# The old state added in PSUM by two 128x64 products instead of one 128x128 product

## The chip, the cores and the metric

The kernel runs on one core of a Trainium2 chip. The metric is device time in microseconds (us) of one execution, and the time of a kernel is the median of its runs. The engines are PE (TensorE, matrix products into PSUM; PEld is its loading of the stationary operand), DVE (VectorE), ACT (ScalarE), POOL (GpSimd) and SP (which issues the DMAs). Each engine works through its own list of instructions in order.

## What is computed

A recurrent attention, whose output is the input of two feed-forward blocks, one after the other:

```
for t in range(S):                       # S = 768, 32 heads of 40
    y[:, :, t] = einsum('bhd,bhde->bhe', r_t, state)
    Sa = einsum('bhde,bhe->bhd', state, a_t)
    state = state * w_t - outer(Sa, b_t) + outer(v_t, k_t)
x = y as tokens                          # 3072 x 320
x = leaky(x @ w_in) @ w_out              # width 2048
out = (sigmoid(x @ w_gate) * (x @ w_val)) @ w_out2   # width 1536
```

## The kernel before

**Attention** goes by chunks of 64 steps. Twelve chunks make six blocks `n` of two chunks `ci`; the chunk is `k = 2n + ci`. `q` is one of four batches, with eight heads in it (`i` of four, `h` of two; `h` chooses the lower or upper 64 partitions). For each of the 48 pairs (k, q) the generator `recur` runs one step of the recurrence, and `together` runs two q side by side. A step is a chain across engines, with these lines:

- `fp` (L352): products of the state in FL with r; DVE multiplies them by a mask into W (L355).
- `pm` (L361): eight products of 64 output rows with W; ACT (L365) and DVE (L367) bring them back into W, for each h.
- `yp` (L374, L377, L380): one PSUM tile of 128 partitions by 4 x 104 columns. Columns 40 to 103 are the outputs of the chunk, columns 0 to 39 the new state. L374 adds FL times r (128x64 operands, one for each h, so the product writes 64 of the 128 partitions). L377 adds the old state ST by a product with the whole 128x128 identity into all 128 partitions and 160 columns. L380 adds W times G (128x64 operands, h by turns).
- DVE scales the new state (L384) and writes the outputs y (L395); PE transposes the state (L389), ACT copies it into FL (L391), and ACT and DVE copy it into the next W (L347).

L377 runs when there is a next chunk: 11 chunks by 4 q are 44 of them. All operands are 32-bit floats, and such a product stands in the trace as two passes, so 88.

Around these steps stands other work of the attention: scores `sc` (L190) and transposes `tr` (L216, L225) of the block after the next, the inverses' products `m` (L284, L290) and `qp` (L299), DVE scans `c` and `rc` (L149, L155) of the block after the next. Late in each block, between its last two pairs of steps, DVE transposes the inverse of the next block (`TTc` L262, `Ta` L264) and `Ld` for the one after it (`T` L240); this place is called a block end here; POOL works out the inverses in between.

**The feed-forward blocks** follow. x is loaded (L556, L558) and split into high and low halves `xh`, `xl` on ACT and DVE (L574 to L577). Weights come as 64-bit numbers and are decoded on DVE, ACT and POOL (L510 to L525), beside the products `h` and `o` (L593, L609). The tile x has one buffer, and the decoding of all weights but the first is put behind the output y of (k = 11, q = 2).

The order of instructions on each engine is set by a scheduler that runs over the whole program and goes by its own estimate of each instruction's time. So an edit of one line can move others, on every engine.

Of the kernel before, what the change touches and what calls it, by code (L numbers as in the profile page):

```python
# [18 lines left out]
B, H, S, D = 4, 8, 768, 40  # L19
# [15 lines left out]
def attention(ctx, tc, A, xT, prods):  # L35


    nc = tc.nc
# [8 lines left out]
    ident = const.tile([128, 128], FP32, name="ident")  # L47
# [264 lines left out]
    def bank2(n, name, shape):  # L312
        if n == NB - 1 and name in ('fp',):
            return pa.tile(shape, FP32, tag="pa", name=name)
        return pf.tile(shape, FP32, tag="pf", name=name)
# [3 lines left out]
    def by8(x):  # L319
        return x.rearrange("p e (u x) -> p e u x", x=8)  # L320
# [4 lines left out]
    def recur(n, q, ci):  # L325
# [6 lines left out]
        FL, ST = st["S", k, q]  # L332
# [10 lines left out]
        if more:  # L343
            for h in range(2):
                nc.sync.dma_start(out=W[top[h], h, 0:D // 8], in_=A["v"][h, :, k, q])
            for h in range(2):
                (nc.scalar.copy if h else nc.vector.tensor_copy)(  # L347
                    out=we[own[h].start:own[h].start + ns[h], h, :, 0:D // 8], in_=by8(ST[64 * h:64 * h + ns[h], :, 0:D]))
        fp = bank2(n, "fp", [128, 8, C])
        for h in range(2):  # L350
            for j in range(2):
                nc.tensor.matmul(out=fp[:, 4 * h + 2 * j:4 * h + 2 * j + 2], lhsT=both(FL[:, j, 2 * h:2 * h + 2]),  # L352
                                 rhs=R[:, :, 2 * h + j], start=True, stop=True)
# [6 lines left out]
        for h, i, e in heads:  # L360
            nc.tensor.matmul(out=pm[own[h], i, cols], lhsT=QT[rows[h], 2 * (i // 2) + h, i % 2], rhs=W[rows[h], h, u0:, i],  # L361
                             start=True, stop=True)
# [8 lines left out]
        yp = bank2(n, "yp", [128, 4, X1])  # L371
        for j in range(2):
            for h in range(2):
                nc.tensor.matmul(out=yp[64 * h:64 * h + 64, 2 * j:2 * j + 2, D:X1], lhsT=FL[:, j, 1 + h],  # L374
                                 rhs=R[:, :, 2 * h + j], start=j == 0, stop=False)
        if more:
            nc.tensor.matmul(out=yp[:, :, 0:D], lhsT=ident, rhs=ST[:, :, 0:D], start=False, stop=False)  # L377
        for h, i, e in heads:
            g0 = D * (2 * i + h)
            nc.tensor.matmul(out=yp[64 * h:64 * h + 64, i, cols], lhsT=Gt[:, g0:g0 + 64], rhs=W[:, h, u0:, i],  # L380
                             start=False, stop=i == 3)
# [14 lines left out]
        if ci == 1:  # L396
            for h in range(2):
                nc.sync.dma_start(
                    out=xT.rearrange("(h f e) t -> f e h t", f=2, e=D)[h][:, :, q * S + n * PB:q * S + n * PB + PB],
# [9 lines left out]
    def together(*chunks):  # L409

        todo = [recur(*x) for x in chunks]
        while todo:
            for x in todo:
                for _ in range(4):
                    next(fill[0], None)
            todo = [x for x in todo if next(x, todo) is not todo]
# [500 lines left out]
```

## Time and profile before

| | us |
|---|---|
| median of 3 runs (1250.61 to 1257.71) | 1252.32 |
| the profiled execution | 1257.15 |
| its span, first to last instruction | 1255.4 |
| PE busy in the span | 1149.8 |
| DVE busy in the span | 735.7 |

The attention fills the span up to about 480 us. From there to 600 us the first pass of the first feed-forward block runs, which also decodes weights, and then the rest. The mean granted PE clock is 0.952 of full speed (2.4 GHz); the two levels are 1.2 and 2.4 GHz, so a stretch at 0.90 spent a fifth of its time at the lower one.

### The profile page before, as it was taken

What the parts mean: (1) busy time and instruction counts of PE and PEld (TensorE: products, weight loads), DVE (VectorE), ACT (ScalarE), POOL (GpSimd) and SP (SyncE); (2) the same over time, 40 slices, a digit from 0 to 9 for tenths busy, and PEclk for the clock granted to TensorE, in tenths of its full rate; (3) what the DMA queues carried; (4) which work ended last, traced back from release to release, by engine and by line L of the source; (5) the groups of instructions that cost most, each with busy time, mean ns of one, the idle gap of its engine ahead of it and who ended that gap; (6) DMA issues with size and microseconds to landing.
All of it is one profiled execution on the core that took longest, in us unless ns stands there. A gap on an engine that the chain in (4) does not pass through costs nothing.

```text
span 1255.4 us, 24949 instructions
## 1 busy us (share of the span) xinstructions
PE 1149.8 (92%) x9778; PEld 970.1 (77%) x9778; DVE 735.7 (59%) x1477; ACT 540.2 (43%) x1214; POOL 327.4 (26%) x528
## 2 busy tenths in 40 slices
PE   4749999999999878998999999999999999999997
PEld 3637878787788766876778888877878888888886
DVE  8975667758655247999964444689762323222222
ACT  2334545445454434676653334467651323222221
POOL 6338481845854002444200000022210000000000
PEclk9659899899999887999999999999999999999999
DMA  6503333333322134333420000146850100000000
GB/s 195 172 23 96 95 88 106 80 103 97 92 50 65 29 106 119 93 103 111 124 72 22 26 21 26 43 122 170 186 130 1 46 1 22 1 22 1 21 1 24
DMA packets 121214, 91.08 MB, mean 73 GB/s; under 512 B 57728, under 2 KB 104320, under 8 KB 121088
## 3 DMA queue, kind: packets, MB, share of 16 engines
q1 hardware_dynamic: 121088, 89.40, 26.1%
q8 instruction: 79, 1.29, 0.4%
q14 instruction: 47, 0.39, 0.1%
HBM read 77.57 MB, written 11.80 MB: 71 GB/s over the span
## 4 chain that ended last, share of the span: by engine, by line
PE 66%; DVE 17%; DMA 6%; ACT 4%; issue 4%; SPq 1%; POOL 1%; DVEq 0%; ACTq 0%
PE h L593 18%; PE o L593 9%; PE o L609 9%; PE qp L299 4%; PE pm L361 4%; PE o L716 3%; PE o L717 3%; PE o L718 3%; PE yp L380 3%; PE fp L352 3%; PE sc L190 2%; PE yp L374 2%; DVE c L149 2%; PE m L290 2%; DMA ru<-in_w_val 2%
## 5 line engine op out<-in xcount | busy, mean ns | idle before, releaser
L593 PE MATMUL h<-xh,up 128*128 128x512 f32 x624 | 200.4, 396 | 10.5 <-DVE g L601 8.9
L593 PE MATMUL h<-xl,up 128*128 128x512 f32 x624 | 194.2, 392 | 0.0
L583 ACT CAST gh<-g 128x512 fp32r<-128x512 f32 x168 | 103.9, 619 | 174.1 <-DVE g L729 113.8
L584 DVE TENSOR_TENSOR gl<-g,gh 128x512 fp32r<-128x512 f32 x168 | 122.7, 732 | 71.5 <-ACT gh L583 71.3
L729 DVE TENSOR_TENSOR g<-o,t 128x512 f32<-128x512 f32 x72 | 49.5, 690 | 187.4 <-PE o L593 184.5
L593 PEld LDWEIGHTS h<-xh,up 128*128 128x128 f32 x624 | 115.7, 189 | 38.9 <-DVE g L601 15.5
L593 PEld LDWEIGHTS h<-xl,up 128*128 128x128 f32 x624 | 117.7, 189 | 23.7
L609 PE MATMUL o<-gh,down 128*128 128x512 f32 x450 | 133.3, 390 | 0.2
L525 POOL TENSOR_TENSOR down<-f,e 128x256 fp32r<-128x256 f32 (+2 forms) x41 | 40.8, 1010 | 228.9 <-PE o L609 172.4
L601 DVE TENSOR_TENSOR g<-h,t 128x512 f32<-128x512 f32 x96 | 65.9, 687 | 58.1 <-ACT t L600 57.6
L609 PEld LDWEIGHTS o<-gh,down 128*128 128x128 f32 x450 | 84.5, 188 | 18.6 <-ACT gh L583 1.1
L254 POOL TENSOR_TENSOR T<-T,tmp 128x30 f32<-128x30 f32 (+9 forms) x150 | 92.9, 620 | 10.9
L725 ACT ACTIVATE t<-h 128x512 f32<-128x512 f32 x72 | 42.9, 597 | 121.9 <-PE h L593 121.8
L593 PE MATMUL o<-xh,up 128*128 128x512 f32 x288 | 89.7, 391 | 3.7 <-DVE g L729 1.6
L609 PE MATMUL o<-gl,down 128*128 128x512 f32 x270 | 92.3, 390 | 0.3 <-DVE gl L584 0.2
L249 POOL TENSOR_TENSOR tmp<-T 128x30 f32<-128x30 f32 (+9 forms) x150 | 87.1, 581 | 10.8
L593 PE MATMUL o<-xl,up 128*128 128x512 f32 x288 | 88.6, 389 | 0.0
L600 ACT ACTIVATE t<-h 128x512 f32<-128x512 f32 x96 | 56.9, 592 | 63.0 <-PE h L593 62.8
L525 POOL TENSOR_TENSOR up<-f,e 128x384 fp32r<-128x384 f32 x38 | 46.2, 1216 | 130.9 <-DVE e L519 129.2
L717 PE MATMUL o<-down,gh 128*128 128x320 f32 x264 | 80.3, 308 | 0.0
L716 PE MATMUL o<-down,gh 128*128 128x320 f32 x264 | 80.0, 309 | 0.0
L367 DVE TENSOR_TENSOR W<-pm,masks 64x256 f32<-64x256 f32 x96 | 40.5, 422 | 62.5 <-ACT W L365 60.4
(267 smaller groups left out, 2254.5 us busy)
## 6 DMA issues: line engine op xcount, KB each, us to landing
kb<-in_kb SPq DMA_DIRECT2D x24, 512.0 KB
rd<-in_w_out SPq DMA_DIRECT2D x28, 320.0 KB
w<-in_w SPq DMA_DIRECT2D x24, 260.5 KB
FL<-in_vT SPq DMA_DIRECT2D x96, 64.0 KB
ru<-in_w_in SPq DMA_DIRECT2D x16, 384.0 KB
x<-in_w SPq DMA_DIRECT2D x24, 256.0 KB
ru<-in_w_gate SPq DMA_DIRECT2D x12, 384.0 KB
ru<-in_w_val SPq DMA_DIRECT2D x12, 384.0 KB
```

The lines of the kernel that those rows point to most:

```text
L249: eng.tensor_tensor(out=tv, in0=T[:, i0:i1, j:j + 1].to_broadcast([128, i1 - i0, j]), in1=T[:, j:j + 1, 0:j].to_broadcast([128, i1 - i0, j ...
L254: steps.append(eng.tensor_tensor(out=T[:, i0:i1, 0:j], in0=T[:, i0:i1, 0:j], in1=tv, op=ALU.add))
L299: nc.tensor.matmul(out=qp[:, 2 * j + h], lhsT=X[:, 2 * ci + j, 2 * h:2 * h + 2].rearrange("p a s -> p (a s)"), rhs=tt[:, 4 * h + 2 * ci + ...
L525: nc.gpsimd.tensor_tensor(out=out, in0=f[:, c0:c1], in1=ef[:, c0:c1], op=ALU.mult)
L583: copy = self.nc.scalar.copy(out=gh, in_=g)
L584: self.last = copy.ins, (engine or self.nc.vector).tensor_tensor(out=gl, in0=g, in1=gh, op=ALU.subtract).ins
L593: self.nc.tensor.matmul(out=ps, lhsT=l, rhs=r, start=(i == 0), stop=(i == len(ops) - 1))
L600: self.nc.scalar.activation(out=t, in_=h, func=AF.Copy, scale=0.01)
L601: self.nc.vector.tensor_tensor(out=g, in0=h, in1=t, op=ALU.max)
L609: self.nc.tensor.matmul(out=acc, lhsT=l, rhs=r, start=first and i == 0, stop=last and i == len(ops) - 1)
L716: nc.tensor.matmul(out=o, lhsT=gj, rhs=w[:, 0], start=s, stop=False)
L717: nc.tensor.matmul(out=o, lhsT=gj, rhs=w[:, 1], start=False, stop=False)
```

## The change

The product with the identity is made in two halves: for each h the 64 columns of the identity that give the output partitions 64h to 64h + 63. The values are the same, in the same place of the same accumulation.

```diff
         if more:
-            nc.tensor.matmul(out=yp[:, :, 0:D], lhsT=ident, rhs=ST[:, :, 0:D], start=False, stop=False)
+            for h in range(2):
+                nc.tensor.matmul(out=yp[64 * h:64 * h + 64, :, 0:D], lhsT=ident[:, 64 * h:64 * h + 64], rhs=ST[:, :, 0:D],
+                                 start=False, stop=False)
```

Lines behind the edit have numbers that are higher by two in the changed kernel (L380 is L382 there), and the halves stand on L378. Up to the first of these products the lists of all engines are as before. Behind it the scheduler has moved other instructions, of which three places are shown.

PE, at the two steps of chunk k = 2 with q = 2 and q = 3, in the trace from 208.8 us. `FL_127` and `S_126` belong to one q, `FL_129` and `S_128` to the other; before:

```order
L374 MATMUL yp<-R_119,FL_127 64x2x64 x4
L377 MATMUL yp<-S_126,ident 128x4x40
L380 MATMUL yp<-W,G_101 64x104 x8
L374 MATMUL yp<-R_120,FL_129 64x2x64 x4
L377 MATMUL yp<-S_128,ident 128x4x40
L380 MATMUL yp<-W,G_103 64x104 x8
L216 MATMUL tr<-ident,a_107 128x104 x4
```

and of the changed kernel:

```order
L374 MATMUL yp<-R_119,FL_127 64x2x64 x4
L378 MATMUL yp<-S_126,ident 64x4x40 x2
L382 MATMUL yp<-W,G_101 64x104 x8
L374 MATMUL yp<-R_120,FL_129 64x2x64 x4
L378 MATMUL yp<-S_128,ident 64x4x40 x2
L382 MATMUL yp<-W,G_103 64x104
L216 MATMUL tr<-ident,a_107 128x104 x4
L225 MATMUL tr<-ident,kb 128x104 x4
L382 MATMUL yp<-W,G_103 64x104 x7
```

The halves stand where the whole stood. Behind them transposes have moved in among the products of the second q.

DVE, at the end of the same block (the three long transposes, in the trace from 213.1 us); before:

```order
L264 STREAM_TRANSPOSE Ta<-T 128x32x32
L347 COPY W<-S_122 40x4x5x8
L347 COPY W<-S_132 40x4x5x8
L240 STREAM_TRANSPOSE T<-Ld 128x32x32
L355 TENSOR_TENSOR W<-fp,masks 128x4x8x8 x4
L367 TENSOR_TENSOR W<-pm,masks 64x4x8x8 x4
```

and of the changed kernel:

```order
L264 STREAM_TRANSPOSE Ta<-T 128x32x32
L347 COPY W<-S_122 40x4x5x8
L347 COPY W<-S_132 40x4x5x8
L355 TENSOR_TENSOR W<-fp,masks 128x4x8x8 x2
L240 STREAM_TRANSPOSE T<-Ld 128x32x32
L355 TENSOR_TENSOR W<-fp,masks 128x4x8x8 x2
L367 TENSOR_TENSOR W<-pm,masks 64x4x8x8 x4
```

The mask products of one q have moved ahead of the third transpose. The same holds at three of the block ends (139.6, 213.1 and 350.1 us); at the one at 286.3 us it was so before.

ACT, at the end of the attention (in the trace from 455 us), where the first x is split; before:

```order
L365 ACTIVATE W<-pm 64x4x5x8 x2
L576 CAST xl_7130<-x 64x512
L365 ACTIVATE W<-pm 64x4x5x8
L510 ACTIVATE sq<-rd 128x320
L391 COPY FL_131<-st__6340 128x2x2x40
L574 CAST xh_7129<-x 128x1536
L365 ACTIVATE W<-pm 64x4x5x8
```

and of the changed kernel:

```order
L365 ACTIVATE W<-pm 64x4x5x8 x3
L512 ACTIVATE sq<-rd 128x320
L578 CAST xl_7174<-x 64x512
L393 COPY FL_131<-st__6384 128x2x2x40
L365 ACTIVATE W<-pm 64x4x5x8
L576 CAST xh_7173<-x 128x1536
```

The third and the fourth copy of `pm` each stand ahead of a half of the split that was ahead of them. Further on in that place, the last copy into FL has moved ahead of the split of the second x on ACT, and the last pair of mask products (L355) ahead of it on DVE.

## Rows read from the trace of the kernel before

**Rows 1.** The page, part 4: the chain that ended last, by engine.

```profile
PE 66%; DVE 17%; DMA 6%; ACT 4%; issue 4%; SPq 1%; POOL 1%; DVEq 0%; ACTq 0%
```

**Rows 2.** Busy time by stretch: stretch, length, engines' busy us, PEclk, DMA share, GB/s.

```profile
100.00:480.00 380.00, 343.41 (x5327) 290.16 (x5325) 230.22 (x480) 176.84 (x511) 187.38 (x330) 0.93 0.32 84
480.00:600.00 120.00, 115.14 (x531) 91.94 (x529) 115.12 (x250) 78.73 (x168) 48.35 (x45) 0.97 0.38 108
600.00:1255.00 655.00, 636.78 (x3087) 541.84 (x3086) 305.56 (x534) 252.66 (x441) 41.72 (x36) 1.00 0.19 51
```

**Rows 3.** Timeline of PE, chunk k = 2: start, us, line, operands, passes [idle before].

```profile
208.81 0.61 PE L374 MATMUL yp<-R,FL 128*64 128x128 f32 x8
209.35 0.54 PE L377 MATMUL yp<-S,ident 128*128 128x160 f32 x2
209.81 0.94 PE L380 MATMUL yp<-W,G 128*64 128x104 f32 x16
```

**Rows 4.** The chain in order of time: start, us on the chain, what, passes.

```profile
208.98 0.44 PE yp L374 x8
209.42 0.47 PE yp L377 x2
...
394.52 1.81 PE fp L352 x16
```

**Rows 5.** Timeline of PE where L380 follows L374 with nothing between.

```profile
224.81 0.66 PE L374 MATMUL yp<-R,FL 128*64 128x128 f32 x8
225.30 0.34 PE L380 MATMUL yp<-W,G 128*64 128x104 f32 x2
```

**Rows 6.** Timeline of DVE, chunk k = 2, q = 0: the second half of W.

```profile
172.37 0.42 DVE L367 TENSOR_TENSOR W<-pm,masks 64x256 f32<-64x256 f32 x1 [2.09 <-ACT W L365]
```

**Rows 7.** Timeline of PE at that time.

```profile
172.37 0.54 PE L377 MATMUL yp<-S,ident 128*128 128x160 f32 x2
172.84 0.30 PE L380 MATMUL yp<-W,G 128*64 128x104 f32 x1
```

**Rows 8.** Timeline of DVE at two block ends.

```profile
213.14 2.02 DVE L262 STREAM_TRANSPOSE TTc<-T 128x1024 f32<-128x1024 f32 x1
...
217.45 2.02 DVE L240 STREAM_TRANSPOSE T<-Ld 128x1024 f32<-128x1024 f32 x1
219.29 1.46 DVE L355 TENSOR_TENSOR W<-fp,masks 128x256 f32<-128x256 f32 x4
...
290.64 0.76 DVE L355 TENSOR_TENSOR W<-fp,masks 128x256 f32<-128x256 f32 x2
291.31 2.07 DVE L240 STREAM_TRANSPOSE T<-Ld 128x1024 f32<-128x1024 f32 x1
293.26 0.74 DVE L355 TENSOR_TENSOR W<-fp,masks 128x256 f32<-128x256 f32 x2
```

**Rows 9.** Timeline of PE at the same two block ends.

```profile
219.81 1.26 PE L361 MATMUL pm<-W,QT 104*64 104x104 f32 x16 [0.95 <-DVE W L355]
...
291.12 1.26 PE L361 MATMUL pm<-W,QT 104*64 104x104 f32 x16 [0.75 <-DMA FL<-in_vT]
...
293.72 0.30 PE L361 MATMUL pm<-W,QT 104*64 104x104 f32 x1 [0.32 <-DVE W L355]
```

**Rows 10.** Busy time by stretch, 17 us from the same block ends on.

```profile
213.10:230.10 17.00, 15.70 (x200) 13.40 (x198) 11.82 (x18) 9.32 (x27) 9.34 (x23) 0.90 0.42 121
286.30:303.30 17.00, 14.85 (x230) 12.54 (x229) 14.41 (x24) 11.44 (x32) 8.93 (x19) 1.00 0.47 127
```

**Rows 11.** Timeline of ACT at the end of the attention.

```profile
462.12 0.62 ACT L576 CAST xl<-x 64x512 fp32r<-64x512 f32 x1 [6.07 <-DMA x<-xT]
462.77 0.30 ACT L365 ACTIVATE W<-pm 64x160 f32<-64x160 f32 x1
```

**Rows 12.** Timeline of DVE at the end of the attention.

```profile
478.43 0.69 DVE L577 TENSOR_TENSOR xl<-x,xh 64x512 fp32r<-64x512 f32 x1
479.15 0.76 DVE L355 TENSOR_TENSOR W<-fp,masks 128x256 f32<-128x256 f32 x2
481.85 0.43 DVE L395 TENSOR_TENSOR y<-yp,c 128x256 f32<-128x256 f32 x1 [1.94 <-PE yp L380]
482.19 0.55 DVE L512 SCALAR_TENSOR_TENSOR z<-sq,ru 128x384 f32<-128x384 f32 x1
```

## Prediction

> **What bounds the kernel now.** I read the page's chain of waits first. PE holds 66% of it and DVE 17% [rows 1], so the first question at each place is what PE would do a little earlier. The table by stretch [rows 2] splits the span. The changed product runs only between 100 and 480 us. There PE is busy for 343.4 of 380 us at a mean granted clock of 0.93. From 480 to 600 us PE and DVE are both near full (115 of 120 us each), and the work of both is fixed there, so this stretch should neither give nor take much if it starts earlier. From 600 us on PE alone is full at clock 1.00, and nothing of it is touched. So what is saved before 480 us should reach the end, if PE or what follows from PE ends last where it is saved.
>
> Then I read the timeline and the chain around one of the 44 products. The L377 rows stand on the chain with 0.47 us each [rows 4]. 44 of these are 21 us, of which only a part can go, since the addition itself stays.
>
> **The direct saving.** The neighbours L374 and L380 use the 128x64 form (all rows, half the columns of the array), L377 the whole array. What the form costs is seen in four differences.
>
> - Eight passes of L374, each over 128 columns, hold the chain for 0.44 us, and sixteen of fp (whole array, also 128 columns) for 1.81 us [rows 4]. That is 0.055 against 0.113 us for a pass: passes for the two halves run side by side.
> - From the start of L374 to that of L377 are 0.54 us [rows 3]. The passes explain 0.44, so 0.10 us pass before the array takes the other form.
> - From the start of L377 to that of L380 are 0.46 us [rows 3].
> - Behind an L377, L374 needs 0.49 us until L380 starts [rows 5], 0.05 more than the 0.44 without a change of form ahead of it. I take this for the first weights, whose loading nothing covers.
>
> So where a 128x64 product follows, an L377 costs 0.10 + 0.46 + 0.05 = 0.61 us. Its replacement is four passes of 160 columns in a stream that never changes its form: 4 x 0.055 x 160/128 = 0.28 us. The saving is 0.33 us. Where another form follows (a score, an inverse's product), the leaving costs what entering cost before: 0.56 us become 0.28 + 0.10, and 0.19 is saved. By the new order of PE, 31 of the 44 are followed by a 128x64 product, 11 by a smaller form, and 2 by a whole-array product, where I take nothing. That is 31 x 0.33 + 11 x 0.19 = 12.3 us of PE time.
>
> Not all of it is on the path. At k = 2, q = 0 the second half of W ends at 172.79 us [rows 6] and L380, which reads it, starts at 172.84 [rows 7]. PE could start 0.05 us earlier, and about 0.28 of the 0.33 turns into a wait for DVE. I count five such places by comparing each L380 with its W, and take 1.5 us off: **about 11 us**. As bounds I take 6 (half of the saving turns into such waits) and 13.5 (nothing does, and the few products at the lower clock save twice as much).
>
> The product's operands don't change: ST and the identity are ready where they were ready, no wait is added, and no DMA is moved by the edit itself. PSUM holds the same tile. The 44 extra instructions on PE are in the passes already counted.
>
> **What the new order does.** Three things that I price apart from the saving.
>
> *Block ends.* DVE stands there in three long transposes. In the order before at 213 us, the mask products of both q come behind the third transpose (219.29), and pm waits 0.95 us for them. At 286 us one pair comes ahead of the third transpose (290.64 against 291.31), and pm starts behind it, with 0.75 us of waiting for a DMA and then 0.32 for the other pair [rows 8, 9]. Behind the first kind the granted clock is 0.90 over 17 us, behind the second 1.00 [rows 10]; that is 3.4 us at the lower level, worth up to 1.7 us if PE ends last all that time. The change turns three ends of the first kind into the second. Each can gain nothing (the waits of the second kind are as long) or 0.95 + 1.7 = 2.6 us. I take 1 us each, nearer to the low end because transposes move in among the yp products there too, which puts off y and so the DVE transposes: **3 us**, bounds 0 and 7. The later third transpose delays POOL's inverse by one pair, 0.76 us [rows 8]. In no row does a TTc wait for POOL, so this is free.
>
> *Scans.* At one block the mask products come earlier among the DVE scans than before, and at the next block later. The two are mirror images, and I price them at nothing, with the wait of 0.95 us [rows 9] each way as bounds.
>
> *The handover.* On ACT, a copy of pm stood behind a split that waited 6.07 us for the first x; it ran at 462.77 [rows 11]. On DVE the last mask products stood behind the split of the second x and ran at 479.15, and y, which releases the decoding of the weights, at 481.85 [rows 12]. In the new order both are ahead of the splits. y still stands behind the split of the second x, which ends at 479.12 [rows 12], so this alone gives at most 2.7 us, and an earlier first split, which frees the buffer of x, up to 2 more by my estimate from the queue on ACT. But x must still land, and six lists of instructions have to agree. I take **2 us**, bounds -2 and 5.
>
> **The sum.** 11 + 3 + 2 = 16 us off the profiled execution of 1257.15 us (span 1255.4, and 1.75 us around it): 1241.15. That execution was 0.4% slower than the median of 1252.32; in the same ratio the forecast is 1241.15 x 1252.32 / 1257.15 = **1236 us**. The bounds are 6 + 0 - 2 - 1 = 3 us and 13.5 + 7 + 5 + 1 = 26.5 us off, 1249 and 1226 in medians.
>
> **The rivals.**
>
> *Only the direct saving.* The three effects of order come to nothing, since what waits is moved and not removed, as the DMA wait in [rows 9] shows. 11 us off: 1241.
>
> *PE's time turns into waits.* W is the limit at many more steps than I counted: pm, ACT and DVE make a chain of their own, which the faster PE does not shorten. For it speaks [rows 7], against it the 0.47 us for an L377 on the chain [rows 4]. 3 to 5 us off at the most: 1248.
>
> *The halves don't run side by side, slower.* The two halves read the same ST through the same rows of the array. If each pass ran alone, four would take 4 x 0.113 x 160/128 = 0.57 us, about the 0.56 of now, and if each also had to load its weights with nothing running (0.05 us [rows 5]), 0.77 us. Then a site with a 128x64 successor loses 0.16 us and any other 0.31: 31 x 0.16 + 13 x 0.31 = 9 us slower, 1261 if the order gives nothing. It decides from 0.14 us for each pass on. Against it speaks [rows 4]: the halves of L374 use the same rows of the array, too, and keep 0.055 us, which leaves no room for loads.
>
> The Trainium skill has a rule for this: its page "TensorE: Matmul & The Clock Gate", section "Part 3: Packing small matmuls — row/col tiling", says that weight loads overlap running products only when the row groups differ. By this rule the two column halves would load unhidden, and the time would be this rival's; the L374 rows of this trace disagree.
>
> **How the numbers follow.** Forecast (direct saving and some of the order's) 0.45; only the direct saving 0.30; waits 0.18; halves one by one, or an order that costs more than the saving, 0.07. About 0.5%, 6.3 us, is what a measurement of this kernel can tell from no change. Faster than 1246.1 are the first two cases and a small part of the third, less a part of the second whose direct saving is at its lower bound: 0.77. Slower than 1258.6: 0.05. The rest is 0.18. The range 1227 to 1248 takes in the first two cases with their bounds and the edge of the third.
>
> **What would show it.** In the profile after, each pair of halves should hold the chain for about 0.28 us with no gap before L378 and L382, and its four passes should start two by two. The waits of pm for W (L355) at the three block ends should shrink and the clock there stay at 1.00. The first z of the later weights, at 482.19 us now [rows 12], should start near 466, and the distance from there to the end should stay within 3 us. The prediction is wrong if L378 passes are more than 0.14 us apart, if waits of L382 for W appear for as much as the products lost, or if the feed-forward part gets longer by what the attention gave.

## The result, and the profile after

| | before | after |
|---|---|---|
| median, first comparison | 1251.46 us (4 runs) | 1234.46 us (4 runs) |
| ratio, 95% interval | | 0.9866 [0.9819, 0.9913] |
| the same again on another occasion | 1255.55 us (17 runs) | 1236.25 us (6 runs) |
| ratio, 95% interval | | 0.9858 [0.9812, 0.9905] |
| the profiled execution | 1257.15 us | 1242.24 us |

The changed kernel is faster by 1.3 to 1.4%, clear of the 0.5% that a measurement can tell. The forecast was 1236 us. The two profiled executions differ by 14.9 us. This is where these lie, by stretches that begin and end at the same instructions: the first L374, the first z on DVE (it decodes the first weights), and on ACT the first copy of an output of the first feed-forward block into x2 by L655 (L657 in the changed kernel). [rows 12] ends with another z, the first one of the later weights; the two are kept apart below.

Busy time by stretch of the kernel before (stretch, length, busy us of PE, PEld, DVE, ACT, POOL, then PEclk, DMA share, GB/s):

```profile
100.07:459.96 359.89, 333.81 (x5261) 282.52 (x5259) 218.13 (x454) 169.04 (x495) 185.31 (x327) 0.95 0.32 84
459.96:612.48 152.52, 137.16 (x652) 109.84 (x648) 137.27 (x299) 94.02 (x198) 54.19 (x51) 0.92 0.37 104
612.48:1255.40 642.92, 624.30 (x3032) 531.50 (x3030) 295.49 (x512) 245.16 (x426) 37.89 (x33) 1.00 0.19 51
```

and of the changed kernel:

```profile
106.94:442.60 335.66, 312.63 (x5349) 274.37 (x5347) 220.17 (x454) 168.13 (x496) 191.31 (x327) 0.97 0.34 90
442.60:595.04 152.44, 137.41 (x649) 109.54 (x646) 138.69 (x298) 93.85 (x197) 52.69 (x51) 0.93 0.37 104
595.04:1240.50 645.46, 626.57 (x3035) 534.20 (x3033) 295.42 (x514) 245.76 (x427) 35.98 (x33) 0.99 0.19 50
```

Until the first L374 the changed kernel takes 6.9 us more (106.94 against 100.07), although no instruction has moved there. The recurrence, where the 44 products stand, is 24.2 us shorter at a higher clock. From the first z to the first x2 nothing changes (152.52 and 152.44), and the rest is 2.5 us longer. 6.9 - 24.2 - 0.1 + 2.5 = -14.9.

**The products themselves**, one step of chunk k = 2 and the start of the next, timeline of PE of the changed kernel (start, us, line, operands, passes), to be read against [rows 3]:

```profile
206.37 0.61 PE L374 MATMUL yp<-R,FL 128*64 128x128 f32 x8
206.81 0.44 PE L378 MATMUL yp<-S,ident 128*64 128x160 f32 x4
207.08 0.88 PE L382 MATMUL yp<-W,G 128*64 128x104 f32 x16
207.79 0.61 PE L374 MATMUL yp<-R,FL 128*64 128x128 f32 x8
```

From L374 to the halves are 0.44 us (0.54 before), from the halves to L382 0.27 (0.46 before), and to the next L374 0.71 (0.77 before, 209.81 to 210.58).

**A block end**, the one at 213 us before; DVE and then PE of the changed kernel, to be read against [rows 8, 9] (in brackets the idle time ahead and what ended it):

```profile
215.48 0.76 DVE L355 TENSOR_TENSOR W<-fp,masks 128x256 f32<-128x256 f32 x2
216.15 2.07 DVE L240 STREAM_TRANSPOSE T<-Ld 128x1024 f32<-128x1024 f32 x1
218.13 0.70 DVE L355 TENSOR_TENSOR W<-fp,masks 128x256 f32<-128x256 f32 x2
...
215.96 1.26 PE L361 MATMUL pm<-W,QT 104*64 104x104 f32 x16 [0.71 <-DVE W L355]
218.56 0.30 PE L361 MATMUL pm<-W,QT 104*64 104x104 f32 x1 [0.32 <-DVE W L355]
```

The wait of 0.95 us has become two that are together as long, 0.71 and 0.32. At the other two ends of the first kind one wait of 1.02 and one of 1.01 us became 0.51 and 0.54.

The clock over 17 us at the three block ends of the first kind, of before (the one at 213.1 us is in [rows 10] with 0.90):

```profile
139.60:156.60 17.00, 15.70 (x189) 13.42 (x186) 10.51 (x18) 8.51 (x25) 9.26 (x24) 0.80 0.41 118
350.00:367.00 17.00, 15.63 (x199) 13.35 (x198) 11.31 (x19) 9.37 (x27) 8.97 (x21) 0.90 0.19 45
```

and from the same three ends of the changed kernel on; the fourth row is its end that was of the other kind already (at 286.3 us before, at 274.2 now), and the last row begins 12 us behind the start of that end:

```profile
144.60:161.60 17.00, 16.42 (x251) 14.57 (x249) 15.12 (x26) 11.69 (x33) 8.94 (x19) 1.00 0.52 147
211.20:228.20 17.00, 14.99 (x240) 12.99 (x239) 14.93 (x25) 11.91 (x33) 8.99 (x19) 1.00 0.49 132
339.60:356.60 17.00, 16.40 (x250) 14.55 (x248) 10.84 (x19) 11.61 (x32) 8.39 (x21) 1.00 0.26 67
274.20:291.20 17.00, 16.41 (x250) 14.56 (x249) 15.11 (x26) 11.68 (x33) 8.92 (x19) 1.00 0.52 147
286.30:303.30 17.00, 14.72 (x218) 13.32 (x215) 14.66 (x22) 9.19 (x24) 15.66 (x18) 0.90 0.19 47
```

At all three the clock stays at full speed now. A second trace of the kernel before (r1 below) has it at 1.00, 1.00 and 0.80 over 17 us from the same three ends, so a fall there does not come each time. Over all traces of this document it came at 16 of 19 ends of the first kind, and at 4 of 23 that the new order, or the same exchange by itself, had turned into the second.

The fall in the last row, at 296.4 us, stands in the scans, which the forecast called mirror images. PE's wait for the masks behind them stood at 237.82 us in the kernel before and stands one block later, at 295.69 us, in the changed one (first row before, second after):

```profile
237.82 1.83 PE L361 MATMUL pm<-W,QT 104*64 104x104 f32 x16 [2.55 <-DVE W L355]
...
295.69 1.68 PE L361 MATMUL pm<-W,QT 104*64 104x104 f32 x16 [2.28 <-DVE W L355]
```

**The handover**, DVE of the changed kernel, to be read against [rows 12]:

```profile
458.72 0.42 DVE L397 TENSOR_TENSOR y<-yp,c 128x256 f32<-128x256 f32 x1
459.06 0.55 DVE L514 SCALAR_TENSOR_TENSOR z<-sq,ru 128x384 f32<-128x384 f32 x1
```

The first z of the later weights has come from 482.19 to 459.06 us. That is 23.1 us earlier, or 30.0 if both are counted from the first L374. The end is 14.9 us earlier.

### The profile page after: what moved, and what is told of

Its sections match the earlier page's. It is cut to its first block, busy times and chain, and to the rows that moved or that the text cites. A ratio compares the mean times of both kernels' runs of the same rounds, so it can differ in the third digit from the quotient of the medians.

```text
span 1240.5 us, 25118 instructions
## 1 busy us (share of the span) xinstructions
PE 1131.1 (91%) x9866; PEld 964.3 (78%) x9866; DVE 746.0 (60%) x1477; ACT 539.7 (44%) x1214; POOL 329.9 (27%) x528
## 4 chain that ended last, share of the span: by engine, by line
PE 43%; DVE 9%; DMA 4%; issue 3%; ACT 2%; POOL 1%; SPq 0%; DVEq 0%; ACTq 0%; POOLq 0%
PE h L595 17%; PE o L595 9%; PE o L611 7%; PE o L718 3%; PE o L719 3%; PE o L720 3%; DVE gl L586 2%; DVE z L514 1%; DVE g L603 1%; DMA ru<-in_w_val 1%; POOL down L527 1%; DVE u L516 1%; DVE e L521 1%; DMA ru<-in_w_gate 1%; DVE f L522 1%
## 5 line engine op out<-in xcount | busy, mean ns | idle before, releaser
L595 PEld LDWEIGHTS h<-xl,up 128*128 128x128 f32 x624 | 118.2, 190 | 23.9
L254 POOL TENSOR_TENSOR T<-T,tmp 128x30 f32<-128x30 f32 (+9 forms) x150 | 95.7, 638 | 11.1
L190 PE MATMUL sc<-kb,a 40*32 40x128 f32 x1536 | 51.9, 323 | 31.4 <-DVE kb L168 25.4
```

The source lines that it names most:

```text
L190: nc.tensor.matmul(out=scs[h][64 * f + 32 * u:64 * f + 32 * u + 32, 2 * ci + j].rearrange("p a s -> p (a s)"), lhsT=a[d, ci, i, 32 * u:32 ...
L254: steps.append(eng.tensor_tensor(out=T[:, i0:i1, 0:j], in0=T[:, i0:i1, 0:j], in1=tv, op=ALU.add))
L595: self.nc.tensor.matmul(out=ps, lhsT=l, rhs=r, start=(i == 0), stop=(i == len(ops) - 1))
```

## The experiments

Fourteen traces are compared below, two of each kernel that a reader has seen and ten of others. Several kernels hold the order of instructions fixed: when the program has been written out, a table gives the row wanted for each engine's queue (its list of instructions), and each instruction is tied to the one ahead of it by an edge that orders and does not wait. "Old row" is that of the kernel before, "new row" that of the changed kernel.

```diff
         experts(c2, tc, A, xT, x2T, out, last, bad)
+    issue_order(tc)
...
+        row = [i for k in seq for i in mine[k]]
+        for a, b in zip(row, row[1:]):
+            tc.add_manual_dep(b, a.name, mybir.DependencyInfo(mybir.DependencyClass.NoSync, mybir.DependencyReason.DATA),
+                              reason="issue_order")
```

All readings stand in one table, in us. "At 1.2 GHz" is the time that the granted clock spent at its lower level in the stretch before it, and "rest" is the stretch less half of that. The half is an estimate of what the lower clock took; it is exact where PE works through all of it. "z" is the first z, at 459.96 us in the kernel before; the expectations of e1, e2 and e3 count to the later one instead, at 482.19.

| label | products | row | L374 to z | at 1.2 GHz | rest | z to x2 | x2 to end | that L152 |
|---|---|---|---|---|---|---|---|---|
| before | whole | old | 359.9 | 37.5 | 341.1 | 152.5 | 642.9 | 0.63 |
| r1 | whole | old | 353.6 | 27.3 | 340.0 | 151.1 | 642.0 | 0.63 |
| e1 | halves | old | 347.1 | 34.1 | 330.0 | 150.4 | 642.6 | 7.57 |
| o1 | halves | old, block ends new | 340.2 | 23.9 | 328.2 | 150.0 | 641.3 | 7.57 |
| o2 | halves | old, handover new | 342.6 | 23.9 | 330.6 | 148.1 | 643.3 | 0.63 |
| e2 | whole | new | 346.7 | 13.7 | 339.8 | 152.8 | 644.1 | 0.63 |
| after | halves | new | 335.7 | 17.1 | 327.1 | 152.4 | 645.5 | 7.57 |
| r2 | halves | new | 335.2 | 17.1 | 326.6 | 151.9 | 644.8 | 7.57 |
| f1 | halves | new | 335.0 | 17.1 | 326.4 | 152.8 | 646.1 | 0.17 |
| e3 | halves | new to handover | 334.8 | 17.1 | 326.3 | 149.7 | 644.3 | 7.57 |
| b1 | halves | new to handover | 335.2 | 17.1 | 326.7 | 151.3 | 645.0 | 0.17 |
| b2 | halves | as b1, block 1 old | 346.1 | 34.1 | 329.1 | 150.5 | 642.9 | 0.17 |
| d1 | halves twice | old | 362.8 | 44.4 | 340.6 | 150.7 | 643.7 | 7.57 |
| d2 | whole twice | old | 366.8 | 27.3 | 353.1 | 149.9 | 644.4 | 0.63 |

The edges by themselves cost nothing that shows: with the new row, the stretch from L374 to z is 334.8 to 335.2 us with them (e3, f1, b1) and 335.7 and 335.2 without (the changed kernel and r2).

### e1: the halves, in the old row

The edit is that of the change, with the second half tied to the first, and the old row on all queues.

> The two halves of the identity in place of the whole product, and nothing else: order-only edges hold every instruction of all five queues in the row in which the kernel before has it, the second half right behind the first. Theory A (the halves shorten each of the 44 sites by the two turns of the array that fall away, and what is more than that came from the new order): first L374 to the first z of the later weights 382.1 -> about 370 us, first z to the end unchanged within 2 us, 11 to 13 us in all, ratio 0.990 to 0.991. Theory B (the halves alone shorten waits behind them, and the 30 us of that stretch are theirs): the stretch at 355 or less, ratio 0.980 or less. Theory C (the saving at a site is mostly hidden by waits for VectorE in a fixed order): the stretch at 378 or more, ratio 0.996 or more.

Measured: median 1245.37 us, ratio 0.9886 [0.9844, 0.9927]. The stretch is 347.1 us. Against one profile of before that is 12.8 us less, against the other 6.6, and the difference between the two is the clock. With it taken out, 330.0 stands against 341.1 and 340.0, so 10.0 to 11.1 us for the 44 sites. Theory A holds: the products alone give what was reckoned site by site, and not the 24 us of the stretch. Counted to the later z as the theories do, 382.1 became 366.4 us, a little beyond A, and from there to the end 773.2 became 773.7, as in A.

### e2: the whole product, in the new row

```diff
+            nc.tensor.matmul(out=yp[:, :, 0:D], lhsT=ident, rhs=ST[:, :, 0:D], start=False, stop=False)
...
+    issue_order(tc)
```

> The whole 128x128 product of the kernel before, with every queue held in the row of the changed kernel: the order by itself. Theory A (order and halves add up): first L374 to the first z 382.1 -> about 364 us (the 30 us less the 12 of the halves), and first z to the end some 6 to 8 us longer as in the changed kernel, so 10 us less in all, ratio 0.991 to 0.993. Theory B (the 30 us are the halves'): the stretch within 3 us of 382, the end 6 to 8 us later, ratio 1.000 to 1.006. A third, C (an order made for quicker sites does harm with slow ones): the stretch over 385.

Measured: median 1246.96 us, ratio 0.9951 [0.9914, 0.9988]. The stretch is 346.7 us, 7 to 13 us less than before with the old product. With the clock taken out almost nothing is left: 339.8 against 341.1 and 340.0. What the row gave here is clock, 13.7 us at 1.2 GHz against 37.5 and 27.3. So A holds in sign and in sum, since 0.49% and e1's 1.14% make 1.63% where both together measured 1.34 and 1.42%, but the 10 us that it wanted in all were too many for a ratio of 0.9951. In its own count A came out: to the later z 382.1 became 363.7 us, and from there to the end 773.2 became 779.8, 6.6 us lost. Most of both is that this z has moved ahead by itself, from 22.2 to 17.1 us behind the first z: counted from the first z, the way to the end is only 1.5 and 3.8 us longer than in the two traces of before.

### d1 and d2: the price of the products by themselves

```diff
-            for h in range(2):
+            for u, h in ((0, 0), (0, 1), (1, 0), (1, 1)):
                 half = nc.tensor.matmul(out=yp[64 * h:64 * h + 64, :, 0:D], lhsT=ident[:, 64 * h:64 * h + 64],
```

> The halves issued twice at each site, all in the row of the kernel before; the old state is added twice, which is wrong in value. Read against the halves once in that row: the added work per site is two more halves with no turn of the array between them. Side by side: 0.13 to 0.14 us per pass pair, two pairs, 0.27 us per site, 42 x 0.27 = 11 us at most and some of it hidden, 8 to 12 us; ratio about 0.997 to 1.000. One by one: 0.54 us per site, 20 us or more, ratio 1.006 or more.

and the whole product twice, with `for u in range(2):` ahead of it:

> The whole 128x128 product issued twice at each site, in the row of the kernel before; the old state is added twice, which is wrong in value. The second one adds no turn of the array. Theory A (the saving of the halves is that of the turns, and the product itself costs the same either way): two more passes of 160 columns per site, 0.25 to 0.28 us as with the halves twice, 10 to 12 us beside the kernel before at equal clock, ratio 1.007 to 1.011. Theory D (the 128x128 product is itself the dear one): 0.44 us per site or more, 19 us, ratio 1.015 or more.

Both add the old state twice. Measured: d1 1255.47 us, ratio 0.9992 [0.9948, 1.0037]; d2 1261.27 us, ratio 1.0069 [1.003, 1.0108]. Timeline of PE, d1 and then d2, at the same step as above:

```profile
213.25 0.61 PE L374 MATMUL yp<-R,FL 128*64 128x128 f32 x8
213.69 0.71 PE L378 MATMUL yp<-S,ident 128*64 128x160 f32 x8
214.23 0.88 PE L384 MATMUL yp<-W,G 128*64 128x104 f32 x16
...
207.35 0.61 PE L374 MATMUL yp<-R,FL 128*64 128x128 f32 x8
207.89 0.81 PE L378 MATMUL yp<-S,ident 128*128 128x160 f32 x4
208.63 0.93 PE L383 MATMUL yp<-W,G 128*64 128x104 f32 x16
```

The second pair of halves takes 0.54 - 0.27 = 0.27 us, the second whole product 0.74 - 0.46 = 0.28. Over the whole stretch, clock taken out, it is 340.6 - 330.0 = 10.6 us or 0.24 per site, and 353.1 less 340.0 to 341.1, 0.27 to 0.30 per site. The trace of d1 has 44.4 us at 1.2 GHz, so only its rest is compared. So the same sum costs the same in either form once the array stands in it, and the halves of one site run side by side. What the change saves is the two turns of the array at each site. The Trainium skill's page "TensorEngine Tiling (Array Packing)", section "Tiling Modes", says that a change of tiling mode drains the engine. These rows agree and give its price here: 0.10 us on the way in (0.54 against 0.44), 0.46 - 0.28 = 0.18 on the way out, and 0.05 at the next product.

### o1: the block ends alone

Three exchanges on DVE in the old row: two L355 ahead of L240. Nothing else moves.

> The halves in the row of the kernel before, with one thing of the new row: on VectorE, at the three block ends, the mask products (L355) of one q stand ahead of the third long transpose (L240). Nothing moves on another queue. Theory E (these three exchanges are what the new row gives): the waits of TensorE there go, and the stretches at half clock behind them; from the first L374 to the first z 347.1 us with the halves alone -> 333 to 339, half-clock time in it 34 -> 14 to 24 us; ratio 0.978 to 0.984. Theory F (TensorE's and ScalarE's rows have to move as well, as in the forecast's bound of nothing): 344 us or more, 30 us or more at half clock, ratio 0.987 to 0.990.

Measured: median 1236.87 us, ratio 0.9871 [0.9837, 0.9904]. The stretch is 6.9 us shorter than in e1, between the two theories; the time at 1.2 GHz is in the range of E, the ratio in that of F. 1.8 us of it remain with the clock taken out; 10.2 us less at 1.2 GHz are the other 5.1 us. At the three ends themselves e1 has the clock at 0.90 each time and o1 at 0.90, 1.00 and 1.00, which is 3.4 of the 5.1 us. By the ratios the time is 0.15% better than e1's, inside both intervals. PE's waits at the ends fell to about 0.3 us, but a larger one stands some 14 us behind the exchange at 213 us, at the scans, and the exchange does not take it away (2.36 us in e1, 2.96 here):

```profile
233.41 1.84 PE L361 MATMUL pm<-W,QT 104*64 104x104 f32 x16 [2.96 <-DVE W L355]
```

### o2: the handover alone

The old row, with the new one for the end of the attention on PE, ACT and DVE, from about 365 to 475 us.

> The halves in the row of the kernel before, with the new row of the handover alone on TensorE, ScalarE and VectorE (the copies and mask products of pm ahead of the splits of x). Theory G (the forecast's: the last steps of the attention end earlier, and what follows starts earlier by as much): first feed-forward product 5 to 6 us earlier and the first x2 2 to 6 us earlier than with the halves alone, ratio 0.984 to 0.987. Theory H (VectorE decodes without a pause from the first z on, 150 to 153 us to the first x2 in all ten traces so far, whatever TensorE does): first feed-forward product 5 us earlier, first z to first x2 150 to 153 us again, x2 and the end within 1 us, ratio 0.988 to 0.990.

Measured: median 1237.81 us, ratio 0.989 [0.9856, 0.9924], so level with e1 (0.9886). From the first z to the first feed-forward product pass 12.2 us, 7.8 less than in e1 (441.55 to 453.71 against 453.57 to 473.52), and from z to x2 2.3 less. These 2.3 us may be clock: between z and x2 o2 has 10.2 us at 1.2 GHz, e1 17.1. Theory H, nearly: TensorE starts and then waits for DVE. Timeline of PE, the first feed-forward product and the next h that needs g; o2, then the changed kernel:

```profile
453.71 0.73 PE L597 MATMUL h<-xh,upf 128*128 128x512 f32 x2
463.23 1.22 PE L597 MATMUL h<-xh,up 128*128 128x512 f32 x2 [1.86 <-DVE g L605]
...
457.63 0.73 PE L595 MATMUL h<-xh,upf 128*128 128x512 f32 x2
468.26 1.22 PE L595 MATMUL h<-xh,up 128*128 128x512 f32 x2 [5.41 <-DVE g L603]
```

In all fourteen traces 148.1 to 152.8 us lie between z and x2, whenever TensorE starts. DVE is busy for 137 to 139 of them, and PE, which starts later, for 134 to 138. That DVE is the limit is read from o2, where PE started 7.8 us earlier and x2 came 2.3 us earlier; no run made DVE's part shorter.

### e3, r1, r2, f1, b1, b2

e3 keeps the new row to the handover and has the old one in the first pass:

> The halves, and the changed kernel's row up to and with the handover; from the first 30 decoding steps of the later weights on, all of the first pass and what follows stand in the row of the kernel before. Theory P (the 8 us that the changed kernel gives back between the first z and the end come from its row in the first pass, which sets decoding steps on VectorE ahead of the first g, so that TensorE waits 5.4 us at once): the attention keeps its 30 us, first z to the end comes back to 773 +- 2 us, 28 us less in all, ratio 0.976 to 0.980. Theory Q (VectorE bounds the start of the first pass whatever its row, and an earlier start only finds it still busy): first z to the end stays at 779 or more, ratio 0.984 to 0.988.

Measured: median 1236.68 us, ratio 0.9814 [0.977, 0.9858]. The attention keeps its gain (334.8 us); z to x2 is 149.7, 2.2 to 2.7 us less than in the two traces of the changed kernel, and 794.0 from z to the end against 797.9 and 796.8. Counted from the later z, as in the theories, 778.1 us remain to the end: P wanted 773, Q 779 or more, and the ratio, too, lies between the two. So the new row of the first pass costs some 3 us in the traces, not 8, and even these are not shown to be the row's: between z and x2 e3 has 13.7 us at 1.2 GHz, the changed kernel 20.5 and 17.1. Most of what an early TensorE wins is lost, as Q has it. By the medians e3 and the changed kernel on another occasion (1236.25) are level, and the intervals of their ratios overlap.

The two repeats, without an edit:

> The kernel before once more, for a second trace. Theory K (how often TensorE falls to the lower clock between the first L374 and the first z belongs to the row of instructions: about 37 us at half clock in the kernel before and 34 with the halves in its row, 14 to 17 us in the three runs with the new row as far as the handover): 30 to 45 us at half clock again, at about the same places. Theory L (it is a matter of the single execution): any amount from 14 to 45. And the wait of one L152 on VectorE for the row of memsets on GpSimd (0.63 us here, 7.57 us in all four traces with halves): 0.63 us again if it belongs to the program, either of the two if it is chance.

> The changed kernel once more, for a second trace and a narrower interval. Theory K (clock by the row): 12 to 20 us at half clock from the first L374 to the first z. Theory L (chance): any amount up to 45. The L152 in question at 7.57 us if that belongs to the program. Ratio 0.985 to 0.989.

The kernel before: 1247.81 us, with 27.3 us at 1.2 GHz where its first profile had 37.5, just under what theory K wanted. The changed kernel: 17.1 us, both times, at nearly the same places. Over all traces the old row has 23.9 to 44.4 us (eight, with o1, o2 and b2, where part of it is new), the new row 13.7 to 17.1 (six). They don't overlap, but two executions of the kernel before differ by 10.2 us at 1.2 GHz, 5 us of time, and the eight by up to 20.5. That is K for the rows, and L within the old one.

f1 gives one L152 on DVE two tensor operands:

```diff
-        nc.vector.tensor_scalar(out=last, in0=c.rearrange("p a b s -> p (a b) s")[:, :, C:C + 1],
-                                scalar1=1e-30, scalar2=None, op0=ALU.max)
+        if n == 0 and q == 3:
+            nc.vector.tensor_tensor(out=last, in0=c.rearrange("p a b s -> p (a b) s")[:, :, C:C + 1],
+                                    in1=segv[:, 0:8, 1:2], op=ALU.max)
...
```

> The changed kernel in its own row, with one instruction in another form: the fourth L152 (floor under the products of the decays) reads a second operand, zeros, in place of the constant 1e-30, as the L165, L168 and L207 beside it, which ran while GpSimd's memsets ran; the floor of 1e-30 is left out there. Theory M (that instruction's 7.57 us are a wait for GpSimd's row of memsets to end, and the unprofiled runs have it too): first L374 at 100 in place of 107, 6 to 7 us less in all, ratio 0.980 to 0.982 against 0.986 of the changed kernel. Theory N (only profiled executions have it): the trace shortens, the times don't, ratio within 0.002 of the changed kernel's. Theory O (not that wait): L152 still above 7 us.

Measured: median 1234.17 us, ratio 0.9827 [0.9786, 0.9868]. In the trace the instruction takes 0.17 us and the first L374 comes at 99.12, as forecast. In time the kernel gains 0.3% on the changed one, 3.9 us by the ratios and 2.1 by the medians, with intervals that overlap. That is between M and N.

b1 is e3 and f1 together, b2 has block n = 1 in the old row as well:

> Two things together that each stood alone before: the changed kernel's row to the handover with the first pass in the row of the kernel before, and the fourth L152 with two operands (its floor of 1e-30 left out). Theory M (the wait at L152 is in every execution with halves): 6 to 7 us less than with the row alone, ratio 0.975 to 0.977. Theory N (only under the profiler): the trace 6 to 7 us shorter, the other executions within 2 us, ratio 0.980 to 0.982.

> As the one before it, and the block n = 1 (scores, scans, steps) on all five queues in the row of the kernel before. In the new row the pairs of steps there take 2.0 and 1.9 us more at equal clock than with the halves in the old one (24.4 against 22.4, 18.5 against 16.6). Theory R (these rows are independent places): 2 to 3.5 us less from the first L374 to the first z than without it, 331 to 333 us, ratio 0.002 lower. Theory S (the loss moves: the old row of that block expects a later end of the block before, and makes waits of its own): 334 us or more, and no gain.

Measured: b1 1229.54 us, ratio 0.9811 [0.9767, 0.9854], level with e3's ratio as N has it; b2 1238.94 us, ratio 0.9877 [0.9831, 0.9923]. b2 lost 10.9 us of the stretch (346.1 against 335.2), 2.4 of them with the clock taken out. The choice of the block was a mistake: the piece that went back to the old row begins with the block end at 213 us and the scans behind it, where the new row is the better one, so its gain went with it. The loss of the new row is at the scans of the block after it. b1 has the lowest ratio of all, but its interval overlaps that of the changed kernel; no version is shown to beat it.

## Why the prediction was right, and where not

**The direct saving (11 us).** Right, as to mechanism and size: 10.0 to 11.1 us (e1, clock taken out). Four passes of the halves fill 0.27 us (0.28 forecast), nothing stands idle ahead of L378 or L382, and d1 and d2 show that the saving is that of the turns alone. The rival of halves one by one is excluded: a second pair would have cost 0.54 us and cost 0.27. So is the one of waits that eat PE's gain, with 10.0 to 11.1 us left in e1.

**Block ends (3 us).** The mechanism was right for the clock, which was at 0.80, 0.90 and 0.90 and stays at 1.00, and for the waits at two ends (1.02 and 1.01 to 0.51 and 0.54 us); at 213 us the wait is only split (0.95 to 0.71 and 0.32). The size was too small. The term priced the clock with up to 1.7 us at each end and then took 1 us for wait and clock together. By the rows above, the three windows of before lost 0.20, 0.10 and 0.10 of 17 us to the clock, 6.8 us in all, beside the waits; in r1 they lost 3.4. o1 puts the exchanges by themselves at 5.2 us, 1.8 without the clock and 3.4 by the clock at the three ends. The other 1.7 us by which its stretch is shorter than e1's stand elsewhere and need not be theirs.

**Scans (0 us).** Right in sum, by the wrong bound. A wait of 2.55 us goes at one block and one of 2.28 comes at the next, each with a fall of the clock behind it, where the bounds were 0.95 each way. b2 shows what one side is worth if it is taken alone.

**Handover (2 us).** Its mechanism is half right. TensorE does start earlier, by more than forecast (7.8 us in o2), and it gives at most 2.3 us at x2, which the clock alone could make. The step that failed is the one that let what is saved before 480 us reach the end "if PE or what follows from PE ends last": from the first z to x2 148.1 to 152.8 us pass in all traces, whenever PE starts, with DVE's decoding as the likely limit. So the sign that was named, within 3 us from the first z of the later weights to the end, was wrong: that distance grew from 773.2 to 781.5 us (482.19 to 1255.4, 459.06 to 1240.5), because that z moved ahead without what it leads to. The first z near 466 came at 459.06.

**What the sum left out.** The clock as a term of its own. From the first L374 to the first z, over the two traces of each kernel, 356.8 us became 335.4. Of these 21.4 us, 10 to 11 are the halves, 3 to 4 the new row with the halves (330.0 to 326.3 to 327.1), and 7.7 are half of the 32.4 - 17.1 us less at 1.2 GHz. The 7.7 rest on two traces of a kernel that differ by 5 us in this. Against it stand 6.9 us at one L152 in the profiled execution and 2.5 us behind x2, where the clock falls for 6.8 us at 893.7 us. The forecast of 16 us off is near the 14.9 in the profiles and the 17.0 and 19.3 in the medians partly because these cancel, and that part is luck.

Most falls of the clock stand behind waits of PE. In the changed kernel four of its five falls in that stretch begin 0.6 to 1.8 us after a wait of 1.92 to 2.30 us has ended; in the kernel before four follow waits of 2.00 to 2.65 us and three begin at or just behind the waits of 1.02, 0.95 and 1.01 us at the block ends; two stand behind no wait of that size. In r1 two waits of 0.95 and 0.98 us at block ends have no fall behind them. That fewer waits cause fewer falls is what these rows suggest. No run moved a wait without moving instructions, so it is not shown by itself.

## What to carry to other kernels

Keep neighbouring products in one tiling of the array: here a single 128x128 product between 128x64 ones cost 0.24 us over its own work, and its halves cost no more than the whole. When an edit lets a scheduler set a new order, read the new row for waits of TensorE, and allow with each wait for the clock that may fall behind it. Time saved ahead of a stretch that another engine bounds comes through only as far as that engine's first instruction moves.

## What the runs showed that was not expected

One L152 on DVE, 128 x 8 elements with a constant as second operand, takes 0.63 us in five traces and 7.57 in six. POOL runs a row of memsets at that time. Timelines of DVE, of before, the changed kernel, o2 and f1:

```profile
19.15 0.63 DVE L152 TENSOR_SCALAR prods<-c 128x8 f32<-128x8 f32 x1
...
19.12 7.57 DVE L152 TENSOR_SCALAR prods<-c 128x8 f32<-128x8 f32 x1
...
19.06 0.63 DVE L152 TENSOR_SCALAR prods<-c 128x8 f32<-128x8 f32 x1
...
19.12 0.17 DVE L153 TENSOR_TENSOR prods<-c,seg 128x8 f32<-128x8 f32 x1
```

and of POOL in the changed kernel, the memsets that begin ahead of it and the last:

```profile
18.78 1.84 POOL L91 MEMSET TTx<- 128x1024 f32 x2
...
25.01 1.65 POOL L91 MEMSET X<- 128x192 f32 x8
```

L152 ends at 26.69 us with the last memset (26.66), and in the kernel before at 19.78, just behind where the first of the two memsets of TTx gives way to the second (19.71). So, as these traces read, it waits for a gap in POOL's row, and either slips in between two memsets or waits for all that follow. With two tensor operands it doesn't wait (0.17 us). The Trainium skill's page "SBUF — State Buffer", section "SBUF: two separate sides", has an exclusive lock on a pair of ports that VectorE and GpSimd share, held for the whole instruction; the trace agrees with such a lock, though no run shows that it is this one, and here VectorE stood behind 25 instructions of GpSimd in a row, not behind one. The case of 7.57 us came in all traces with halves and the old form of L152 but o2's, and in none with the whole product; why is open, as in all of them it starts 0.34 us after the first memset of TTx. Open too is how often it comes in unprofiled executions, since f1 and b1 gained 0 to 4 us in time and 7 in the trace, and o2, without it in its trace, has e1's ratio.
